# Moving 58 raw weight loads from SyncE's DMA queue to GpSimd's in a one-core attention and two-network kernel

## The chip, the core and the metric

The kernel runs on one NeuronCore of a Trainium2 chip. The core has a matrix engine (TensorE, in the rows PE), a vector engine (VectorE, DVE), an activation engine (ScalarE, ACT), a general engine (GpSimd, POOL) and SyncE (SP), which in this kernel only issues DMA transfers. Each engine takes its own instructions in order. The metric is the device time of one execution in microseconds (us); lower is better.

## What is computed

Three stages follow one another. Inputs are float32, except that the scaled weights come as float64 and are read by the kernel as pairs of 32-bit words.

```python
# attention: batch 4, 8 heads, 768 positions, head size 64, chunks of 32 with 16 left and 8 right
scores = q_c @ concat(mem_k, k_ctx).T / sqrt(64);  a = softmax(scores);  x = a @ concat(mem_v, v_ctx)
# first network: 3072 tokens, 512 -> 2048 -> 512
h = x @ w_in;  g = h * tanh(softplus(h));  x = g @ w_out
# second network: 3072 tokens, 512 -> 1536 -> 512
xn = x / sqrt(mean(x * x) + 1e-6) * rms_g
out = (silu(xn @ w_gate) * (xn @ w_val)) @ w_out2
```

## The kernel before

All large products are split into a high and a low part of each operand (three matmuls for one product), and most are done by a seven-product block scheme, a `group`. In the text the stages go by the lines of the matmuls:

- to about 300 us: attention, with the first products against `w_in` (`unit`, `group1`, matmuls L639 to L641) woven between its pieces; its results go to `g_scratch` in device memory;
- 300 to 378 us: the rest of `group1`;
- 378 to 645 us: `out1` (matmuls L754 to L756) reads `g_scratch` back through a `Feed` (load L771, activation L782) and multiplies by `w_out`;
- 645 to 985 us: `group2` (L639 to L641 with 512 columns), 36 groups against `w_gate` and `w_val`; operands `T` come from `nt_scratch` (L628), results `s` go to `h_scratch` (L111, through `store_later`);
- from 985 us: `group3` (L909 to L911) against the last `w_out2`.

Within a `group`, ScalarE copies the first bank into a tile `c` (L649), VectorE adds banks into it (L654, L665, L668, L670), and GpSimd adds the last quarter (L669) from `c` and a copy of another bank (L657). The pool of `c` tiles in `group2` has two buffers, so L649 of one group waits until L669 of an earlier one has read the tile.

The weights are converted on the fly by a generator, `cv_all`. A raw tile of 512 KB is loaded by `load_raw` (the DMA is line L149), two words for each value. ScalarE takes both halves (L202, L205), VectorE assembles the value (L209, L210, L216), and the value is split into high and low parts (L153 on ScalarE, L154 on VectorE, or on GpSimd for the rows of `w_out`). The pool `raw` has two buffers: the load of part n + 2 waits until L210 has read part n. `cv_prefetch` asks for the next load as soon as a part is done.

There are 74 such loads. The 16 of kind "half" (`w_in` for the first groups, before 123 us) are issued by GpSimd. The other 58 (6 of `w_in` and 24 of `w_gate` and `w_val`, kind "col"; 28 rows of the two `w_out` arrays, kind "row") are issued by SyncE, in one queue with everything else: attention operands, stores and reloads of `g_scratch`, `nt_scratch`, `h_scratch` and of the converted weights (`wi`, `wg`, `wo`). The order of the instructions on each engine is set by a scheduler that simulates the program; code that is marked with `pin` keeps its program order.

Of the kernel before, what the change touches and what calls it, by code (L numbers as in the profile page):

```python
# [29 lines left out]
def tile_kernel(  # L30
# [15 lines left out]
    nc = tc.nc  # L46
# [89 lines left out]
    def load_raw(arr, kind, f):  # L136
        raw = rawp.tile([128, 512, 2], I32, tag="raw", name="raw")
        if kind == "col":
            src = arr[:, f * 128:(f + 1) * 128].rearrange("(k p) f -> p k f", p=128).bitcast(I32)
            dst = raw.rearrange("p (k f) t -> p k (f t)", k=KC)  # L140
        elif kind == "half":
            i, half = f
            src = arr[256 * half:256 * half + 256, 256 * i:256 * i + 256]
            src = src.rearrange("(k p) f -> p k f", p=128).bitcast(I32)
            dst = raw.rearrange("p (k f) t -> p k (f t)", k=2)
        else:
            src = arr[f * 128:(f + 1) * 128, :].bitcast(I32)
            dst = raw.rearrange("p f t -> p (f t)")
        (nc.gpsimd if kind == "half" else nc.sync).dma_start(out=dst, in_=src)  # L149
        return raw  # L150

    def split(src, hi, lo, eng=None, keep=lambda ins: ins):
# [28 lines left out]
    def cv_prefetch(done):  # L181
        flat = [part for job in jobs for part in job[2]]
        while n_load[0] < min(len(flat), n_raw[0]) and n_load[0] - done < 2:
            raws.append(load_raw(*flat[n_load[0]]))
            n_load[0] += 1
# [1099 lines left out]
```

## Time and profile before

| | us |
|---|---|
| median of 3 runs | 1170.4 |
| lowest and highest of them | 1167.4 to 1171.19 |
| profiled execution, its time | 1169.38 |
| profiled execution, span of its instructions | 1167.6 |
| TensorE busy in the span | 1144.3 |
| VectorE, ScalarE, GpSimd busy | 824.7, 619.6, 180.2 |

The span runs from the first to the last instruction that the profile shows; 1.8 us of the execution's time lie around it. Busy time counts instructions that work; issuing a DMA from SyncE does not count. Releasers of waits are inferred. A TensorE clock of 1.00 in a row is the upper of its two levels (2.4 GHz), 0.5 the lower (1.2 GHz), and a value between is a mean over both.

### The profile page before, as it was taken

What the parts mean: (1) busy time and instruction counts of PE and PEld (TensorE: products, weight loads), DVE (VectorE), ACT (ScalarE), POOL (GpSimd) and SP (SyncE); (2) the same over time, 40 slices, a digit from 0 to 9 for tenths busy, and PEclk for the clock granted to TensorE, in tenths of its full rate; (3) what the DMA queues carried; (4) which work ended last, traced back from release to release, by engine and by line L of the source; (5) the groups of instructions that cost most, each with busy time, mean ns of one, the idle gap of its engine ahead of it and who ended that gap; (6) DMA issues with size and microseconds to landing.
All of it is one profiled execution on the core that took longest, in us unless ns stands there. A gap on an engine that the chain in (4) does not pass through costs nothing.

```text
span 1167.6 us, 22949 instructions
## 1 busy us (share of the span) xinstructions
PE 1144.3 (98%) x9052; PEld 1009.6 (86%) x9052; DVE 824.7 (71%) x1254; ACT 619.6 (53%) x1000; POOL 180.2 (15%) x165
## 2 busy tenths in 40 slices
PE   6899999999999999999999999999999999999998
PEld 4789999999999888888888788888888888999998
DVE  3655798844745876785775755978896857888883
ACT  4566666533545876676674433544454433444441
POOL 2011222310132311011011111111111111000000
PEclk9799999999999999999999999999999999999999
DMA  9889799899488774586599388999899889655431
GB/s 197 176 228 222 184 296 263 235 308 284 159 295 297 257 225 154 181 342 200 175 385 364 157 335 304 336 413 392 306 361 369 304 286 329 193 151 145 145 91 37
DMA packets 213276, 294.20 MB, mean 252 GB/s; under 512 B 104240, under 2 KB 160560, under 8 KB 204336
## 3 DMA queue, kind: packets, MB, share of 16 engines
q1 hardware_dynamic: 210864, 284.34, 73.7%
q0 software_dynamic: 2304, 8.39, 2.3%
q8 instruction: 71, 1.16, 0.4%
q14 instruction: 37, 0.30, 0.1%
HBM read 181.80 MB, written 110.89 MB: 251 GB/s over the span
## 4 chain that ended last, share of the span: by engine, by line
PE 90%; DVE 5%; ACT 2%; DMA 1%; issue 1%; POOL 0%; SPq 0%; ACTq 0%; DVEq 0%; POOLq 0%
PE bk L639 14%; PE bk L640 13%; PE bk L641 13%; PE bk L755 5%; PE bk L756 5%; PE bk L754 5%; PE bk L910 4%; PE bk L911 4%; PE bk L909 4%; PE bkp L639 2%; PE bkp L640 2%; PE bkp L641 2%; PE bkp L755 2%; PE bkp L756 2%; PE bkp L754 2%; PE bkp L457 1%
## 5 line engine op out<-in xcount | busy, mean ns | idle before, releaser
L639 PE MATMUL bk<-T,w 128*128 128x384 f32 (+1 forms) x860 | 315.4, 370 | 2.7 <-ACT s L747 2.1
L640 PE MATMUL bk<-T,w 128*128 128x384 f32 (+1 forms) x860 | 311.4, 362 | 0.0
L641 PE MATMUL bk<-T,w 128*128 128x384 f32 (+1 forms) x860 | 308.1, 362 | 0.0
L639 PEld LDWEIGHTS bk<-T,w 128*128 128x128 f32 x860 | 162.1, 189 | 22.2 <-ACT s L747 2.5
L640 PEld LDWEIGHTS bk<-T,w 128*128 128x128 f32 x860 | 162.2, 189 | 16.5 <-DVE T L154 0.3
L641 PEld LDWEIGHTS bk<-T,w 128*128 128x128 f32 x860 | 161.8, 188 | 15.6
L910 PE MATMUL bk<-w,T 128*128 128x256 f32 x396 | 112.0, 283 | 0.0
L911 PE MATMUL bk<-w,T 128*128 128x256 f32 x396 | 112.0, 283 | 0.0
L909 PE MATMUL bk<-w,T 128*128 128x256 f32 x396 | 112.0, 283 | 0.0
L755 PE MATMUL bk<-T,w 128*128 128x512 f32 x276 | 107.6, 390 | 0.2 <-DVE T L154 0.2
L756 PE MATMUL bk<-T,w 128*128 128x512 f32 x276 | 107.1, 389 | 0.0
L754 PE MATMUL bk<-T,w 128*128 128x512 f32 x276 | 106.7, 389 | 0.0
L669 POOL TENSOR_TENSOR v<-c,v 128x512 f32<-128x512 f32 x36 | 52.2, 1449 | 294.6 <-DVE c L665 235.8
L665 DVE TENSOR_TENSOR c<-bk,c 128x512 f32<-128x512 f32 (+2 forms) x72 | 43.1, 599 | 58.0 <-PE bk L641 45.5
L154 DVE TENSOR_TENSOR T<-s,T 128x1024 fp32r<-128x1024 f32 (+1 forms) x50 | 62.7, 1263 | 29.0 <-ACT T L153 28.9
L649 ACT COPY c<-bk 128x512 f32<-128x512 f32 (+2 forms) x72 | 37.0, 515 | 78.1 <-POOL v L669 32.7
L909 PEld LDWEIGHTS bk<-w,T 128*128 128x128 f32 x396 | 76.0, 192 | 0.1
L910 PEld LDWEIGHTS bk<-w,T 128*128 128x128 f32 x396 | 76.0, 192 | 0.1
L911 PEld LDWEIGHTS bk<-w,T 128*128 128x128 f32 x396 | 76.0, 192 | 0.0
L782 ACT ACTIVATE s<-s 128x1024 f32<-128x1024 f32 x44 | 46.5, 1059 | 33.1 <-DMA s<-g_scratch 33.1
L755 PEld LDWEIGHTS bk<-T,w 128*128 128x128 f32 x276 | 51.8, 188 | 11.4 <-DVE T L154 0.6
L756 PEld LDWEIGHTS bk<-T,w 128*128 128x128 f32 x276 | 51.8, 188 | 10.8
(226 smaller groups left out, 2282.3 us busy)
## 6 DMA issues: line engine op xcount, KB each, us to landing
T<-nt_scratch SPq DMA_DIRECT2D x35, 1024.0 KB
g_scratch<-g SPq DMA_DIRECT2D x64, 384.0 KB
s<-g_scratch SPq DMA_DIRECT2D x46, 512.0 KB
h_scratch<-s SPq DMA_DIRECT2D x36, 512.0 KB
w<-wg SPq DMA_DIRECT2D x10, 1792.0 KB
wg<-w SPq DMA_DIRECT2D x30, 512.0 KB
raw<-in_moe_w_out_dram SPq DMA_DIRECT2D x28, 512.0 KB
nt_scratch<-T SPq DMA_DIRECT2D x14, 1024.0 KB
```

Of the source, the lines that this page charges most:

```text
L154: keep((eng or nc.vector).tensor_tensor(lo, src, hi.bitcast(F32), op=ALU.subtract))
L639: nc.tensor.matmul(ps, whi, xh, start=first and kk == 0, stop=False, **more)
L640: nc.tensor.matmul(ps, whi, xl, start=False, stop=False, **more)
L641: nc.tensor.matmul(ps, wlo, xh, start=False, stop=kk == 1, **more)
L669: nc.gpsimd.tensor_tensor(c22, u3, z5, op=ALU.add)
L754: nc.tensor.matmul(ps, ahi, bhi, start=start, stop=False)
L755: nc.tensor.matmul(ps, ahi, blo, start=False, stop=False)
L756: nc.tensor.matmul(ps, alo, bhi, start=False, stop=stop)
L782: nc.scalar.activation(x, g, self.act)
L909: nc.tensor.matmul(ps, t[:, 0, f], w[:, 0], start=first and f == 0, stop=False, **more)
L910: nc.tensor.matmul(ps, t[:, 0, f], w[:, 1], start=False, stop=False, **more)
L911: nc.tensor.matmul(ps, t[:, 1, f], w[:, 0], start=False, stop=f == HG - 1, **more)
```

## The change

Every raw load is now issued by GpSimd; nothing else in the source differs.

```diff
@@ load_raw @@
         else:
             src = arr[f * 128:(f + 1) * 128, :].bitcast(I32)
             dst = raw.rearrange("p f t -> p (f t)")
-        (nc.gpsimd if kind == "half" else nc.sync).dma_start(out=dst, in_=src)
+        nc.gpsimd.dma_start(out=dst, in_=src)
         return raw
```

So 58 instructions leave SyncE's queue and enter GpSimd's, where the scheduler places them. On SyncE, in the middle of `out1`, two loads of raw weights stood among the reloads of `g_scratch` (L771) and the stores of converted weights (L111 `wg<-w`):

```order
 L771 DMA s<-g_scratch 128x2x512 x2
 L111 DMA wg<-w 128x1024 x2
-L771 DMA s<-g_scratch 128x2x512
-L149 DMA raw<-in_moe_w_gate_dram 128x4x256
-L771 DMA s<-g_scratch 128x2x512 x2
-L149 DMA raw<-in_moe_w_val_dram 128x4x256
-L771 DMA s<-g_scratch 128x2x512
+L771 DMA s<-g_scratch 128x2x512 x4
 L111 DMA wg<-w 128x1024
 L771 DMA s<-g_scratch 128x2x512
```

What moved: the two L149 are gone, and the four L771 follow each other directly. On GpSimd in `group2`, from the last sums of squares (L824, L825) on, the 36 L669 stood alone; the first rows of what stands there now are these (`v` is the tile with the group's last quarter):

```order
 L825 TENSOR_TENSOR w<-w 128x512
-L669 TENSOR_TENSOR v<-c,v 128x512 x36
+L669 TENSOR_TENSOR v<-c,v 128x512 x8
+L149 DMA raw<-in_moe_w_gate_dram 128x4x256
+L149 DMA raw<-in_moe_w_val_dram 128x4x256
+L149 DMA raw<-in_moe_w_gate_dram 128x4x256
+L669 TENSOR_TENSOR v<-c,v 128x512
+L149 DMA raw<-in_moe_w_val_dram 128x4x256
+L669 TENSOR_TENSOR v<-c,v 128x512
+L149 DMA raw<-in_moe_w_gate_dram 128x4x256
+L149 DMA raw<-in_moe_w_val_dram 128x4x256
+L669 TENSOR_TENSOR v<-c,v 128x512
```

What moved: 24 loads now stand between the L669, one or two behind each of most of them from the eighth on. On VectorE the same instructions stand in a slightly different order from about 735 us to 925 us; the first such place (L209, L210 and L216 assemble a value, L668, L654 and L749 belong to a group) is:

```order
 L670 SCALAR_TENSOR_TENSOR v<-bk_85,c 128x512
-L668 TENSOR_TENSOR s<-bk_84,s 128x512
-L749 TENSOR_TENSOR s<-s,v 128x1024
-L216 ISA ca<-ca,lr 128x1024
-L210 SCALAR_TENSOR_TENSOR ca<-raw,ca 128x512
-L654 TENSOR_TENSOR s<-bk_87,c 128x512
+L209 TENSOR_SCALAR ca<-ca 128x512
+L668 TENSOR_TENSOR s<-bk_84,s 128x512
+L749 TENSOR_TENSOR s<-s,v 128x1024
+L216 ISA ca<-ca,lr 128x1024
+L654 TENSOR_TENSOR s<-bk_87,c 128x512
+L210 SCALAR_TENSOR_TENSOR ca<-raw,ca 128x512
```

What moved: L210, which frees a raw tile, stands behind L654 instead of ahead of it, and L209 comes a little later. TensorE's matmuls of two neighbouring groups are interleaved in another order in the same stretch; before 735 us only a handful of rows on any engine but SyncE and GpSimd differ.

## Rows read from the trace of the kernel before

**Rows 1.** The page: span, and busy time of each engine.
```profile
span 1167.6 us, 22949 instructions
PE 1144.3 (98%) x9052; PEld 1009.6 (86%) x9052; DVE 824.7 (71%) x1254; ACT 619.6 (53%) x1000; POOL 180.2 (15%) x165
```

**Rows 2.** Stages: stretch and length, busy us of PE, PEld, DVE, ACT, POOL, clock, DMA.
```profile
122.00:300.00 178.00, 177.57 (x2654) 163.88 (x2654) 129.41 (x244) 95.34 (x184) 35.84 (x39) 1.00 0.87 256
300.00:378.00 78.00, 78.00 (x434) 75.34 (x432) 49.44 (x80) 42.52 (x73) 22.41 (x18) 1.00 0.75 259
378.00:645.00 267.00, 266.02 (x1172) 219.61 (x1172) 193.08 (x249) 185.55 (x233) 38.52 (x26) 1.00 0.72 256
645.00:985.00 340.00, 337.32 (x1492) 279.02 (x1491) 253.26 (x381) 150.86 (x262) 50.96 (x36) 0.99 0.86 324
985.00:1165.00 180.00, 178.37 (x1487) 178.16 (x1485) 133.31 (x171) 72.57 (x112) 12.17 (x13) 1.00 0.46 136
```

**Rows 3.** TensorE's waits from 122 us on: total us, times, longest us.
```profile
PE bk L639 <- ACT s L747: 2.1, 1, 2.1
PE bk L639 <- ACT c L657: 0.6, 1, 0.6
PE bkp L639 <- ACT v L657: 0.6, 1, 0.6
PE bk L489 <- ACT p L476: 0.4, 1, 0.4
...
PE bk L755 <- DVE w L154: 0.2, 1, 0.2
```

**Rows 4.** Waits of SyncE's queue at the raw loads, the largest.
```profile
SPq L149 <- DVE ca L210: 101.7, 40, 7.8
```

**Rows 5.** The raw loads' line: issue time, ns min/median/max; landing times of GpSimd's.
```profile
L149 SPq DMA_DIRECT2D raw<-in_moe_w_out_dram x28: 332/333/1416, 208.2 to 911.0; - x28
L149 POOL DMA_DIRECT2D raw<-in_moe_w_in_dram x16: 722/722/847, 3.1 to 122.3; - x16
L149 SPq DMA_DIRECT2D raw<-in_moe_w_gate_dram x12: 372/383/384, 401.8 to 790.9; - x12
...
DMA to landing us min/median/max: 4.3/5.4/7.2
```

**Rows 6.** Waits on both sides of L669: total us, times, longest us.
```profile
POOL v L669 <- DVE c L665: 235.8, 29, 16.8
...
ACT c L649 <- POOL v L669: 32.7, 8, 7.0
```

**Rows 7.** Raw loads beside L669 in `group2`: start and length in us.
```profile
833.26 4.17 SPq L149 DMA_DIRECT2D raw<-in_moe_w_out_dram  x2
868.60 0.33 SPq L149 DMA_DIRECT2D raw<-in_moe_w_out_dram  x1
...
833.97 1.31 POOL L669 TENSOR_TENSOR v<-c,v 128x512 f32<-128x512 f32 x1 [2.79 <-DVE c L665]
867.80 1.57 POOL L669 TENSOR_TENSOR v<-c,v 128x512 f32<-128x512 f32 x1 [8.31 <-DVE c L665]
...
878.48 0.66 ACT L202 ACTIVATE ca<-raw 128x512 f32<-128x512 f32 x1 [2.54 <-DMA raw<-in_moe_w_out_dram]
```

**Rows 8.** Stages of five us around TensorE's longest wait, columns as in rows 2.
```profile
660.00:665.00 5.00, 2.88 (x14) 2.06 (x12) 5.00 (x7) 3.01 (x4) 0.00 (x0) 1.00 0.24 96
665.00:670.00 5.00, 5.00 (x15) 3.98 (x16) 5.00 (x7) 2.99 (x5) 0.00 (x0) 0.66 0.44 175
```

**Rows 9.** VectorE beside an addition, and beside a raw load, on GpSimd: start, length.
```profile
400.09 1.67 DVE L210 SCALAR_TENSOR_TENSOR ca<-raw,ca 128x512 int32<-128x512 int32 x1
399.63 1.58 POOL L154 TENSOR_TENSOR w<-ca,w 128x512 fp32r<-128x512 f32 x1 [2.24 <-ACT w L153]
...
81.51 0.68 DVE L216 CUSTOM_DVE_ANT_0 ca<-ca,lr 128x1024 uint16<-128x1024 uint16 x1
81.55 0.72 POOL L149 DMA_DIRECT2D raw<-in_moe_w_in_dram  x1 [5.33 <-DMA raw<-in_moe_w_in_dram]
```

## The prediction

> **What bounds the kernel now.** I read the page first, for how much time TensorE does not work. It is busy for 1144.3 of 1167.6 us [rows 1], so 23.3 us are all that any edit can give back without making matmuls faster. Next come the stages, for where those 23.3 us lie. From 122 to 985 us, in which all 58 moved loads are issued (the sixteenth load of GpSimd's starts at 122.3, SyncE's last at 911.0 [rows 5]), TensorE is idle for 0.43 + 0 + 0.98 + 2.68 = 4.1 us, and in the stage behind it for another 1.6 [rows 2]. The remaining 17.6 us lie before 122 us or after 1165 us, where the change touches nothing. Third come TensorE's own waits from 122 us on, to see who ended those 4.1 us: 2.1 us in one piece, two of 0.6, one of 0.4, and no row of the view, from the first to the last, names a DMA [rows 3]. So no transfer, raw load or other, makes TensorE wait directly. VectorE is the next engine, with 253.26 of 340 us in `group2` [rows 2]; GpSimd is at 50.96 there. The kernel is bound by matmuls, and the stretch that the change touches is the one where they are closest to gapless.
>
> **The change part by part.**
>
> *Off SyncE.* 58 issues leave, at 0.33 us (28 of them) and 0.38 (the 24 of `w_gate` and `w_val` and, by the same shape, the 6 of `w_in`), together 28 x 0.33 + 30 x 0.38 = 20.6 us, and with them the waits in front of them: 101.7 us on L210 alone, over 40 loads, 7.8 at the longest [rows 4, 5]. Each of those waits held whatever stood behind it in SyncE's queue: stores, reloads of `g_scratch`, operands `T`. This is the part that could gain. But what stood behind ends on no row of TensorE's waits, so I cost the gain on the path at nothing. The cover is the prefetch distance of these transfers; it is given by TensorE's not waiting for one of them in 863 us, and an earlier issue can only lengthen it. The upper end of the gain is the 4.1 us of rows 2, of which the largest piece is bound otherwise (below).
>
> *Onto GpSimd.* The 16 loads that it issues already take 0.72 us each, with a median and a minimum alike and 0.85 at the most [rows 5]. They are of 256 pieces of 2 KB; the row loads are of 128 pieces of 4 KB, the column loads of 512 of 1 KB, and the trace has neither on this queue. If the time went with the pieces, they would take 0.36 and 1.44; if it is fixed, 0.72. I take 0.72, since minimum and median agree, and the range of the sum is 28 x 0.36 + 30 x 0.72 = 32 us to 28 x 0.72 + 30 x 1.44 = 63 us, with 42 as my value. GpSimd then works 222 us instead of 180.2, under a fifth of the span. What hides it is its own idle time: in `group2` 340 - 51 = 289 us [rows 2], against 24 loads of 0.72, 17 us.
>
> *The new waits on GpSimd.* A load waits there for the raw tile, that is mostly for L210 on VectorE, as it did on SyncE. Behind it now stand L669, the L154 of the `w_out` rows, and the sums L823 to L825; behind L669 wait L649 on ScalarE (the tile `c`) and L749 on VectorE. What matters is whether a load stands ahead of an L669 that could already run. L669 itself waits for VectorE, 235.8 us in all for L665 [rows 6]; so both wait for the same engine, and if the scheduler has them in VectorE's order, the load costs L669 only its issue. I laid the old times against the new order. The load issued at 868.60 now stands ahead of the L669 that began at 867.80: held 868.60 + 0.72 - 867.80 = 1.5 us [rows 7]. The pair of loads begun at 833.26 now stands behind the L669 of 833.97 and loses 833.97 + 1.31 - 833.26 = 2.0 us, on a tile with a conversion or more of time before it is read. I found no larger hold of an L669 than the first. Against that stands how much TensorE can bear: ScalarE's L649 already waits for L669, 8 times and for 32.7 us, once for 7.0 [rows 6], and TensorE has no wait that goes back to it at that length; its waits on ScalarE in rows 3 are 2.1 and shorter. So a hold of 1.5 us is covered more than four times, and I cost the move at nothing on the path, with 0 at the lower end and at the upper end what the first rival gives.
>
> *The transfers themselves.* The bytes and the sixteen engines stay. The load issued at 868.60 was waited for until ScalarE started at 878.48, so it landed 9.9 us after its issue among the transfers of SyncE's queue [rows 7]; GpSimd's landed after 4.3 to 7.2 us, median 5.4, in the first stages [rows 5]. I expect the moved ones nearer to the second. That frees ScalarE for a few us, not TensorE: 0 again, with a gain of at most one of the pieces of 0.6.
>
> *Could a busy VectorE starve the issue?* The rows say: while GpSimd issued a load at 81.55, a VectorE instruction from 81.51 took 0.68, and the load its 0.72; while GpSimd added (L154, from 399.63, 1.58 long), VectorE's L210 from 400.09 took 1.67 [rows 9]. So additions on GpSimd and VectorE's work with two inputs stand in each other's way for about 1 us, and issues do not, in those rows. The Trainium skill ("SBUF — State Buffer", SBUF: two separate sides) warns of just this change: a DMA issued by GpSimd has its descriptors written by that engine, which is locked out while VectorE holds the port that both share, so it should go over SyncE's or ScalarE's queue instead. By the row the sum stays 1169.9; by the rule each issue would be longer by a VectorE instruction, and the sum would move only where that makes a hold too long (the second rival).
>
> *The other order.* From about 735 to 925 us VectorE's and TensorE's instructions stand in another order. The sums are the same; the waits there may differ. In the old order they were a small part of 2.68 us, and 2.1 of it (the one long wait) is before 735, so the new order starts from about 0.6 us of waits, and I take the same, with 0 and one long wait more as the ends.
>
> **The sum.** 1169.38 us of the profiled execution, less 0, plus 0. That execution lies 1.0 under the median of 1170.4, so I predict between the two, 1169.9 us.
>
> **The rivals.**
>
> *Slower: GpSimd's queue is held up.* If the real order of VectorE does not match the simulated one, a load that waits as long as on SyncE, 7.8 us [rows 4], then issues for 0.72, holds L669 for 8.5. That is 1.5 over the 7.0 that is borne; from 7.0 on it decides. The price of a hold on TensorE is more than the wait: behind the one long wait, which ended just before 665, the granted clock was 0.66 over 5 us, a mixture of the lower of its two levels and the upper, a loss of 5 x 0.34 = 1.7 us [rows 8]. So such an event costs 1.5 + 1.7 = 3.2 us. Two of them give 1176; a single one in which the whole 2.1 us of rows 3 is repeated gives 1169.9 + 2.1 + 1.7 = 1173.7. Against it: the holds that I could work out are 2 us or less. Chance 0.14, and 0.05 for the same price from the other order on VectorE alone.
>
> *Slower: the issue is starved.* As a mechanism of this kernel: an issue is lengthened by the 1.0 us by which L210 was lengthened in rows 9, so the hold becomes 9.5, and the event 2.5 + 1.7 = 4.2 us; two give 1178. The Trainium skill's page "SBUF — State Buffer" would have it so. Against it: 16 issues of 0.72 to 0.85, in stages where VectorE was less loaded. Chance 0.04.
>
> *Faster: SyncE's queue was the hidden cause.* All waits from 122 to 985 us vanish, with the low clock: 4.1 + 1.7 = 5.8 us, 1164. For it: 101.7 us of waits in that queue. Against it: the longest wait is for ScalarE's L747, in a stretch from 650 on in which the raw tiles serve the last operand and SyncE has no raw load at all, and VectorE is busy for 5.00 of 5 us right there [rows 8]. Without it 2.0 us remain, within what counts as no change. Chance 0.10.
>
> *The change does not do what it says* can't be: the order shows the loads on the other engine.
>
> **How the numbers follow.** A measurement of this kernel can't tell less than about 0.3%, 3.5 us, from no change. No change has 0.67, with 1166.4 to 1173.4 as its own range; slower 0.14 + 0.05 + 0.04 = 0.23; faster 0.10. For 8 in 10 the range runs from 1166 (which leaves out most of the faster case) to 1176 (two holds).
>
> **What would show it.** Right: GpSimd's L149 about 0.7 us each and GpSimd near 220 us busy; the waits of SyncE's queue shorter by some 100 us; TensorE's busy time and idle time from 122 to 985 us within 2 us of 1144 and 4.1; the wait before 665 still there; L649's wait for L669 about as before. Wrong: a TensorE wait released by ScalarE's L649 or L657 behind an L669 that stood behind a load, with a clock under 1.00 after it; L149 on GpSimd well over 1.4 us; or the wait before 665 gone.

## The result: about 1% slower

| | median us | lowest to highest | ratio to the kernel before, 95% interval |
|---|---|---|---|
| before (in the first and the second measurement) | 1170.03, 1170.19 | 1166.92 to 1172.96 | |
| after, first measurement (6 runs) | 1181.54 | 1175.98 to 1184.29 | 1.0097 [1.0078, 1.0116] |
| after, second measurement (5 runs) | 1180.27 | 1178.93 to 1181.15 | 1.0084 [1.0070, 1.0099] |

The prediction was 1169.9 us, no change, with a range of 1166 to 1176. The change costs 10 to 11.5 us. The page of the kernel after (first measurement, an execution of 1182.16 us) in the lines that answer to [rows 1], with the DMA queues (q1 carries what SyncE issues, q0 what GpSimd issues: packets, MB, share of the sixteen engines' time) and the engines' shares of the chain that ended last:

```profile
span 1180.4 us, 22955 instructions
PE 1146.5 (97%) x9052; PEld 1009.9 (86%) x9052; DVE 820.1 (69%) x1254; ACT 619.1 (52%) x1000; POOL 218.7 (19%) x223
...
q1 hardware_dynamic: 190992, 253.93, 65.3%
q0 software_dynamic: 10656, 38.80, 10.1%
...
PE 82%; DMA 8%; DVE 6%; ACT 3%; issue 1%; POOL 0%; SPq 0%; DVEq 0%; ACTq 0%; POOLq 0%
```

TensorE's busy time hardly changed, and GpSimd's 218.7 us are what was forecast. New is what stands in the chain: DMA has 8% of it; in the chain of before it had 1%. Before, q0 carried 8.39 MB and q1 284.34; the 30.4 MB of the 58 raw loads moved from the one to the other.

The stages, columns as in [rows 2]:

```profile
122.00:300.00 178.00, 177.51 (x2655) 163.93 (x2654) 129.30 (x245) 95.62 (x184) 42.56 (x47) 1.00 0.89 257
300.00:378.00 78.00, 77.57 (x430) 74.75 (x429) 47.94 (x78) 42.14 (x72) 27.02 (x27) 1.00 0.74 252
378.00:645.00 267.00, 262.47 (x1148) 216.79 (x1147) 192.28 (x250) 183.05 (x227) 49.12 (x42) 0.99 0.70 246
645.00:985.00 340.00, 332.13 (x1454) 273.23 (x1453) 240.96 (x370) 146.42 (x256) 65.97 (x60) 0.99 0.85 321
```

TensorE's idle time in these four is 0.49 + 0.43 + 4.53 + 7.87 = 13.3 us, where [rows 2] had 4.1. TensorE's waits there, as in [rows 3]:

```profile
PE bk L639 <- ACT c L657: 4.6, 2, 4.3
PE bkp L639 <- DMA T<-nt_scratch: 3.2, 2, 2.4
PE bk L639 <- DMA T<-nt_scratch: 2.5, 1, 2.5
PE bk L639 <- ACT s L747: 2.1, 1, 2.1
```

The 2.1 us of [rows 3] are still there, as forecast. The other three rows are most of the loss, and two of them name what no row of [rows 3] named: a DMA, the load of an operand `T` by SyncE (L628). They lie at three places.

**Near 380 us**, at the start of `out1`. A row of the chain (start, length), and a row each of ScalarE's and TensorE's timeline (in brackets the idle time before the instruction, and what ended it):

```profile
374.23 8.06 DMA w<-g_scratch
...
382.31 1.06 ACT L782 ACTIVATE sm<-w 128x1024 f32<-128x1024 f32 x1 [4.76 <-DMA w<-g_scratch]
...
383.79 0.69 PE L639 MATMUL bk<-T,w 128*128 128x384 f32 x1 [4.30 <-ACT c L657]
```

The reload of `g_scratch` into the tile `w` (L771) takes 8.06 us from its issue; before it took 4.26. ScalarE's L782 waits for it, L657 stands next in ScalarE's queue (it starts at 383.28), and TensorE waits 4.30 us for L657. The 5 us that follow (columns as in [rows 2]) run at a clock of 0.56, which costs another 2.2 us:

```profile
385.00:390.00 5.00, 5.00 (x15) 4.13 (x14) 3.19 (x5) 4.09 (x7) 4.69 (x4) 0.56 0.36 133
```

**Near 770 us**, in `group2`: the operands' loads on SyncE's queue, the raw loads on GpSimd's, and TensorE behind them.

```profile
757.48 3.18 SPq L628 DMA_DIRECT2D T<-nt_scratch  x3
...
760.32 0.77 POOL L149 DMA_DIRECT2D raw<-in_moe_w_gate_dram  x1 [1.19 <-ACT ca L202]
764.75 0.77 POOL L149 DMA_DIRECT2D raw<-in_moe_w_val_dram  x1
...
773.20 0.50 PE L639 MATMUL bk<-T,w 128*128 128x512 f32 x1 [2.53 <-DMA T<-nt_scratch]
...
757.48 15.68 DMA T<-nt_scratch
```

The load of `T` issued at 757.48 is waited for until 773.20, 15.68 us in the chain. The same place in the kernel before (which is some 7 us ahead when `group2` begins), on SyncE's queue alone, and the stretches of it that hold this place and the next (columns as in [rows 2]):

```profile
749.50 1.90 SPq L628 DMA_DIRECT2D T<-nt_scratch  x2
752.34 0.38 SPq L149 DMA_DIRECT2D raw<-in_moe_w_gate_dram  x1
756.03 1.13 SPq L628 DMA_DIRECT2D T<-nt_scratch  x2
758.20 1.12 SPq L149 DMA_DIRECT2D raw<-in_moe_w_val_dram  x1
...
760.00:800.00 40.00, 40.00 (x179) 33.12 (x178) 27.62 (x44) 17.49 (x32) 4.16 (x3) 1.00 1.03 414
870.00:900.00 30.00, 29.44 (x130) 24.07 (x129) 20.24 (x35) 14.38 (x27) 2.59 (x2) 1.00 1.01 409
```

There the raw load of 752.34 stands behind two loads of `T`, and that of 758.20 behind two more. The last two rows are what I had not asked for: from 760 to 800 and from 870 to 900 us the sixteen DMA engines were fully taken already, at 414 and 409 GB/s, so whatever is served earlier is served at the cost of something else.

**From 882 to 889 us**, in the next round of operands, the two waits on `bkp`: 0.84 and 2.37 us.

How far the program had come at four points (starts of the first and last matmuls of the lines named, in us; L639 multiplies in the first network's groups and in `group2`, L754 to L756 in `out1`, whose first products stand among the last of `group1`, from 322.7 us on before; L909 in `group3`) gives the loss by stage, for every kernel that was run:

| profiled execution of | its time | first L639 | to first L754 | `out1`, to last L756 | `group2`, to first L909 |
|---|---|---|---|---|---|
| before | 1169.38 | 45.3 | 277.4 | 310.7 | 347.0 |
| after | 1182.16 | 46.3 | 277.0 | 317.3 | 352.9 |
| after, second measurement | 1180.45 | 46.1 | 279.0 | 314.3 | 352.9 |
| `w_out` only | 1177.29 | 45.4 | 277.9 | 316.0 | 347.8 |
| `w_gate`, `w_val` only | 1172.79 | 45.5 | 276.8 | 311.6 | 350.2 |
| `w_out2` only | 1172.71 | 44.8 | 276.7 | 311.3 | 351.6 |
| issue only | 1173.63 | 45.4 | 277.9 | 311.5 | 349.9 |
| all but `w_out` | 1175.68 | 45.0 | 276.5 | 311.2 | 354.8 |
| operands too | 1197.53 | 45.3 | 278.9 | 318.4 | 364.8 |
| operands and reloads too | 1188.97 | 45.5 | 277.9 | 317.6 | 358.1 |
| eleven back | 1173.76 | 47.2 | 277.2 | 312.9 | 347.1 |
| `w_in`, `w_out` only | 1170.29 | 45.7 | 277.5 | 313.3 | 345.4 |
| `w_val` only | 1169.18 | 44.6 | 276.9 | 312.1 | 347.3 |
| `w_out2` by ScalarE | 1175.29 | 46.0 | 277.8 | 310.8 | 351.8 |

Single executions of one kernel differ by some 4 us either way, so one row of this table settles nothing by itself; the ratios below do, with the waits at the places named.

### The profile page after: what moved, and what is told of

It is laid out like the page before. It is cut to its first block, busy times and chain, and to the rows that moved or that the text cites. A ratio compares the mean times of both kernels' runs of the same rounds, so it can differ in the third digit from the quotient of the medians.

```text
span 1180.4 us, 22955 instructions
## 1 busy us (share of the span) xinstructions
PE 1146.5 (97%) x9052; PEld 1009.9 (86%) x9052; DVE 820.1 (69%) x1254; ACT 619.1 (52%) x1000; POOL 218.7 (19%) x223
## 3 DMA queue, kind: packets, MB, share of 16 engines
q1 hardware_dynamic: 190992, 253.93, 65.3%
q0 software_dynamic: 10656, 38.80, 10.1%
## 4 chain that ended last, share of the span: by engine, by line
PE 82%; DMA 8%; DVE 6%; ACT 3%; issue 1%; POOL 0%; SPq 0%; DVEq 0%; ACTq 0%; POOLq 0%
PE bk L639 12%; PE bk L640 12%; PE bk L641 12%; PE bk L755 5%; PE bk L756 5%; PE bk L754 5%; PE bk L909 4%; PE bk L911 4%; PE bk L910 4%; DMA T<-nt_scratch 3%; PE bkp L754 2%; PE bkp L755 2%; PE bkp L639 2%; PE bkp L756 2%; PE bkp L640 2%; PE bkp L641 2%
## 5 line engine op out<-in xcount | busy, mean ns | idle before, releaser
L639 PE MATMUL bk<-T,w 128*128 128x384 f32 (+1 forms) x860 | 316.1, 370 | 9.4 <-ACT c L657 4.6
L640 PE MATMUL bk<-T,w 128*128 128x384 f32 (+1 forms) x860 | 311.6, 362 | 0.0
L639 PEld LDWEIGHTS bk<-T,w 128*128 128x128 f32 x860 | 162.3, 189 | 29.9 <-ACT c L657 5.2
L909 PE MATMUL bk<-w,T 128*128 128x256 f32 x396 | 112.2, 283 | 0.1
L756 PE MATMUL bk<-T,w 128*128 128x512 f32 x276 | 107.1, 389 | 0.0
L754 PE MATMUL bk<-T,w 128*128 128x512 f32 x276 | 106.4, 389 | 0.0
L665 DVE TENSOR_TENSOR c<-bk,c 128x512 f32<-128x512 f32 (+2 forms) x72 | 43.0, 598 | 68.9 <-PE bk L641 56.6
L669 POOL TENSOR_TENSOR v<-c,v 128x512 f32<-128x512 f32 x36 | 51.1, 1420 | 214.4 <-DVE c L665 160.1
L154 DVE TENSOR_TENSOR T<-s,T 128x1024 fp32r<-128x1024 f32 (+1 forms) x50 | 62.4, 1256 | 29.1 <-ACT T L153 29.0
L649 ACT COPY c<-bk 128x512 f32<-128x512 f32 (+2 forms) x72 | 36.9, 514 | 75.5 <-POOL v L669 26.4
L909 PEld LDWEIGHTS bk<-w,T 128*128 128x128 f32 x396 | 76.0, 192 | 0.4 <-ACT T L153 0.3
L782 ACT ACTIVATE s<-s 128x1024 f32<-128x1024 f32 x44 | 46.5, 1060 | 34.2 <-DMA s<-g_scratch 33.9
L755 PEld LDWEIGHTS bk<-T,w 128*128 128x128 f32 x276 | 51.8, 188 | 11.5 <-DVE T L154 0.6
L756 PEld LDWEIGHTS bk<-T,w 128*128 128x128 f32 x276 | 51.8, 188 | 10.9
```

What stands on the lines that cost most here:

```text
L154: keep((eng or nc.vector).tensor_tensor(lo, src, hi.bitcast(F32), op=ALU.subtract))
L639: nc.tensor.matmul(ps, whi, xh, start=first and kk == 0, stop=False, **more)
L640: nc.tensor.matmul(ps, whi, xl, start=False, stop=False, **more)
L669: nc.gpsimd.tensor_tensor(c22, u3, z5, op=ALU.add)
L754: nc.tensor.matmul(ps, ahi, bhi, start=start, stop=False)
L755: nc.tensor.matmul(ps, ahi, blo, start=False, stop=False)
```

## The experiments

**The theories.** A: a raw load that stood in SyncE's queue was served behind the operands issued before it. On a queue of its own it is served beside them, in stretches where the DMA engines are full, and the transfer that TensorE or ScalarE needs next lands later by that much. B: GpSimd's issues and waits hold L669 and L154 up (my first two rivals). C: the scheduler's other order does it. D: it is a property of GpSimd's queue, not of a second queue as such.

Where nothing else is said, an experiment changes only the line of `load_raw` that the change touched; the sixteen `half` loads stay with GpSimd in all of them.

### Only the rows of `w_out`

```diff
-        nc.gpsimd.dma_start(out=dst, in_=src)
+        (nc.gpsimd if kind == "half" or arr is w_out else nc.sync).dma_start(out=dst, in_=src)
```

> Of the 58 moved loads only the row loads of w_out (16 of the 28 rows) go over GpSimd's queue; the loads of w_gate, w_val and w_out2 stay on SyncE's. The scheduler's order on ScalarE is then that of before, and TensorE's differs in about 50 lines. Theory A (a raw load on a queue of its own no longer stands behind SyncE's earlier transfers, and is served beside or ahead of them): the reload of g_scratch that is waited for near 380 us lands late again, TensorE idles some 4 us there and runs at the lower clock for some 7 us more, so about 6 to 7 us over before, 1176.5 (ratio 1.005 to 1.006); the waits on T<-nt_scratch near 770 and 885 us are not there. Theory B (GpSimd's issues and waits hold L669 and L154 up): a sixth of the loads in a stage with few L669, so 1170 to 1172, with no wait of over 1 us near 380. Theory C (the scheduler's other order does it): the order is nearly that of before, so 1170.

Measured: median 1169.52 us, ratio 1.0004 [0.9988, 1.0019]. The profiled execution, 1177.29, is the slowest of twelve (the others 1167.66 to 1172.85), and it has the stall, in the chain and in TensorE's timeline:

```profile
374.32 7.67 DMA w<-g_scratch
...
383.48 0.44 PE L639 MATMUL bk<-T,w 128*128 128x384 f32 x1 [3.98 <-ACT c L657]
```

So the place is the one that theory A named and nothing came up at 770 or 885 us, but the size was missed: by the times the stall comes in few executions, and the median of this part alone is not slower. TensorE's instructions stand in the order of before until behind this place, so its own order (theory C) did not make the stall. (The 16 rows are 28% of the 58 loads, not the sixth that the expectation has.)

### Only the columns of `w_gate` and `w_val`

```diff
-        nc.gpsimd.dma_start(out=dst, in_=src)
+        (nc.gpsimd if kind == "half" or arr is w_gate or arr is w_val else nc.sync).dma_start(out=dst, in_=src)
```

> Only the 24 column loads of w_gate and w_val go over GpSimd's queue. Theory A: no stall near 380 us; TensorE waits some 2.5 us for T<-nt_scratch near 770 us, where two raw loads of 512 KB are served beside the operands, so 1172 to 1174 (ratio 1.002 to 1.004). Theory B: most loads in the stage with most L669, so more than half of the 11.5 us, 1176 or over, with waits of ScalarE's L649 for L669 longer than the 7.0 of before. Theory C: the order of the stage from 645 us on differs, 1175 or over without any wait for T<-nt_scratch.

Measured: 1173.87 us, 1.0028 [1.0016, 1.0041]. TensorE, near 770 us of the kernel after:

```profile
764.36 0.50 PE L639 MATMUL bk<-T,w 128*128 128x512 f32 x1 [2.04 <-DMA T<-nt_scratch]
```

As theory A has it, with 2.04 us at the place and no stall near 380 us. In the next round of operands TensorE waits 0.83, 0.68 and 0.82 us more for `T`, which no theory had named. The raw loads of that round are on SyncE's queue here, but at other places in it: SyncE issues them behind the second and the fourth load of `T` (raw loads at 865.14 and 868.19; `T` at 862.88, at 864.62, and two from 866.74), where before they stood behind the fourth and the sixth. So the scheduler's order of one queue can put raw loads ahead of operands too; that this is what cost the 2.3 us is argued, and no run tested it.

### Only the rows of `w_out2`

```diff
-        nc.gpsimd.dma_start(out=dst, in_=src)
+        (nc.gpsimd if kind == "half" or arr is w_out2 else nc.sync).dma_start(out=dst, in_=src)
```

> Only the 12 row loads of w_out2 go over GpSimd's queue. Theory A: no stall near 380 nor near 770 us; TensorE waits some 3 us for T<-nt_scratch near 885 us, so 1172 to 1174 (ratio 1.002 to 1.004). Theory B: 12 issues of 0.55 us cost nothing that can be measured, 1170. Theory C: the order from about 735 us on differs, so 1173 to 1176 with no wait for T<-nt_scratch.

Measured: 1172.06 us, 1.0015 [1.0002, 1.0028]. This is the cleanest pair, since up to this place the execution keeps the times of before within 1 us. First the kernel before, SyncE's queue (its raw load of 868.60 is in [rows 7]), then this one, SyncE's queue, GpSimd's, TensorE, and the chain:

```profile
865.13 0.33 SPq L149 DMA_DIRECT2D raw<-in_moe_w_out_dram  x1
871.04 0.32 SPq L628 DMA_DIRECT2D T<-nt_scratch  x1
```

```profile
862.60 7.18 SPq L628 DMA_DIRECT2D T<-nt_scratch  x5
...
865.04 0.74 POOL L149 DMA_DIRECT2D raw<-in_moe_w_out_dram  x1 [6.12 <-DVE ca L210]
867.15 0.55 POOL L149 DMA_DIRECT2D raw<-in_moe_w_out_dram  x1 [1.37 <-ACT w L153]
...
875.07 0.50 PE L639 MATMUL bkp<-T,w 128*128 128x512 f32 x1 [2.62 <-DMA T<-nt_scratch]
...
861.30 13.73 DMA T<-nt_scratch
```

The raw loads are issued at 865.04 and 867.15, where they were issued at 865.13 and 868.60, and the last load of `T` 1 us earlier than before (the five end by 869.78; before the last began at 871.04). No `T` was issued later (the one waited for, the second of the round, at 861.30; before at 861.87), and yet TensorE waits 2.62 us for it, where before it did not wait. TensorE's instructions stand in the order of before until about 886 us, so its own order (theory C) did not make this wait. What changed about these transfers is the queue on which the two raw loads stood, and the trace has what the queues moved from 868 to 876 us, before and then here (packets, MB, share of the sixteen engines' time):

```profile
q1 hardware_dynamic: 536, 3.43, 102.0%
...
q1 hardware_dynamic: 386, 2.25, 69.6%
q0 software_dynamic: 285, 1.04, 32.0%
```

Before, SyncE's queue had the engines for itself. Here the two raw loads, 1.04 MB, took 32% of 8 us, 2.6 us, while TensorE waited for a load of `T` that had been issued 4 and 6 us ahead of them. That is theory A's mechanism in numbers.

### The issue on GpSimd, the bytes on SyncE

```diff
-        nc.gpsimd.dma_start(out=dst, in_=src)
+        for q_, lo, hi in ((nc.gpsimd, 0, 8), (nc.sync, 8, None)) if kind != "half" else ((nc.gpsimd, 0, None),): q_.dma_start(out=dst[..., lo:hi], in_=src[..., lo:hi])
```

> GpSimd issues all the moved loads and waits for their raw tiles as after the change, but each of them moves only the first 8 words of every piece; SyncE's queue issues the rest of the bytes, as before. Theory A: the bytes stand behind SyncE's earlier transfers again, so the waits on T<-nt_scratch near 770 and 885 us and the stall near 380 us shrink to under 1 us each: 1170 to 1173 (ratio 1.000 to 1.003). Theory B: GpSimd's issues and waits are those of after, so 1180 to 1183 (ratio 1.0097).

Measured: 1172.20 us, 1.0019 [1.0004, 1.0034]. GpSimd is busy for 216.7 us and its L149 take as long as after, so theory B's cost is all there, and about four fifths of the loss are gone. The reload near 380 us and TensorE's waits from 645 us on:

```profile
373.23 4.42 DMA w<-g_scratch
...
PE bk L639 <- ACT s L747: 2.7, 2, 2.1
PE bk L639 <- DVE c L665: 1.6, 2, 0.8
```

No wait for `T` is left; 4.42 us for the reload is nearly the 4.26 of before. The 1.6 us for VectorE's L665 are two waits of 0.79, which may be the other order or the doubled loads. Theory B falls. Theory C does not fall by this run, since the scheduler's order here is another again; against it stands the run before, with TensorE's old order and the wait.

### The change again, and all but `w_out`

The first is the changed kernel itself; the second:

```diff
-        nc.gpsimd.dma_start(out=dst, in_=src)
+        (nc.sync if arr is w_out else nc.gpsimd).dma_start(out=dst, in_=src)
```

> The changed kernel itself, once more and on the chip of the other runs of this call. The parts alone added 0.04, 0.28 and 0.15%, 5.5 us together, but the whole 11.5. Theory A1 (the rest is the stall near 380 us, which came in the profiled execution of the w_out part but in none of the other eleven, and comes more often with all parts moved): the times fall into two clusters, one near 1175.5 and one 6 to 7 us above it, with the upper one the more frequent. Theory A2 (the rest is an interaction that is there each time): one cluster near 1181.5. Theory A3 (the chip of the first measurement was another): a median near 1176.

> All moved loads go over GpSimd's queue but the 16 rows of w_out, which stay on SyncE's. Theory A (order of service, place by place): no stall near 380 us, the waits for T<-nt_scratch near 770 and 885 us are there, so 1175 to 1176.5 (ratio 1.004 to 1.0055). If the rest of the loss is an interaction elsewhere than near 380 us: 1180 or over.

Measured: 1180.27 us, 1.0084 [1.0070, 1.0099], five runs within 2.3 us of each other, so one cluster; and 1176.61 us, 1.0049 [1.0031, 1.0068], as theory A had it (1.78 + 1.06 us for `T` near 770, 2.90 near 885, none near 380). The guess of two clusters (A1) fell: the second profiled execution of after, 1180.45 us, has no 4 us stall near 380 (its longest wait between 300 and 400 us is 0.99), but the waits in `group2` again, the last of them now on ScalarE's L205:

```profile
771.91 0.50 PE L639 MATMUL bk<-T,w 128*128 128x512 f32 x1 [2.40 <-DMA T<-nt_scratch]
882.21 0.50 PE L639 MATMUL bkp<-T,w 128*128 128x512 f32 x1 [1.11 <-DMA T<-nt_scratch]
887.45 0.47 PE L639 MATMUL bkp<-T,w 128*128 128x512 f32 x1 [2.19 <-ACT lr L205]
```

Both executions have `group2` at 352.9 us. In `out1` the second lost 3.6 us, with no single wait of TensorE's over 1 us.

### The operands on GpSimd's queue too, and the reloads

```diff
-            nc.sync.dma_start(out=t.bitcast(F32), in_=dram[:, p - 1].bitcast(F32))
+            nc.gpsimd.dma_start(out=t.bitcast(F32), in_=dram[:, p - 1].bitcast(F32))
```

and, in the second kernel, also

```diff
-                nc.sync.dma_start(out=g, in_=self.source(*self.steps[self.nl]))
+                nc.gpsimd.dma_start(out=g, in_=self.source(*self.steps[self.nl]))
```

> As after the change, but the loads T<-nt_scratch of L628 are issued by GpSimd too, so that raw loads and operands stand in one queue again. Theory A: the waits for T<-nt_scratch near 770 and 885 us are gone, the stall near 380 us stays where it comes, so 5 to 6 us under after, 1175 to 1177; near 1170 in executions without that stall. Theory B (GpSimd's queue is held up): a load of T waits there for its tile, L669 behind it is held longer, so 1182 to 1186.

> As the kernel with T<-nt_scratch on GpSimd's queue, and the reloads of g_scratch (L771) there too, so that everything that TensorE waits for after 380 us stands in one queue with the raw loads, and only stores and the loads of other stages are on SyncE's. Theory A: all three stalls gone, 1168 to 1172. Theory B: more waits on GpSimd's queue, L154 and L669 held, 1182 or over.

Measured: 1189.53 us, 1.0174 [1.0141, 1.0207], and 1188.22 us, 1.0163 [1.0137, 1.0188]. Both numbers of theory A missed, by 12 us and more, and those of theory B (over 1182) were nearer. But the traces do not show B's mechanism, an L669 held by a load. In the first kernel no row of TensorE's waits names `T` any more, as A had it; the longest wait is another. ScalarE, TensorE and the chain there:

```profile
957.11 1.02 ACT L153 CAST w<-ca 128x256 fp32r<-128x256 f32 x3 [5.07 <-DMA wo<-w]
...
958.66 0.80 PE L639 MATMUL bkp<-T,w 128*128 128x512 f32 x1 [5.70 <-ACT v L657]
...
940.83 16.18 DMA wo<-w
```

Now a store of converted weights (`wo<-w`, L111 on SyncE) is late, 16.18 us; ScalarE's L153 waits for its slot, L657 stands behind it, and TensorE waits 5.70 us. ScalarE's L649 waits 33.2 us for L669, 8 times and 7.0 at the longest, which is what [rows 6] had. While the store was under way, from 941 to 957 us, GpSimd's queue had 61.9% of the sixteen engines' time. Read so, it is theory A's mechanism with the sides changed: what stayed on SyncE's queue is now served beside what left it. That is argued from this trace, and no further run tested it. It is also one wait of several: another of 3.65 us, at 864.24, ends on ScalarE's L649 behind an L153 that had waited 3.86 us for VectorE, not for a transfer, and near 380 us TensorE waits 3.47 us behind a reload of 7.22. The second kernel still has 2.00 us for `T` and 2.23 for a converted weight (`w<-wg`), and near 380 us, where reload and raw loads now stand in one queue, a wait of 3.24 us on ScalarE's L153. So theory A does not account for the 8 to 9 us that these two kernels take beyond the changed one.

### Eleven of the 58 back on SyncE's queue

```diff
-        nc.gpsimd.dma_start(out=dst, in_=src)
+        back = arr is w_out and f in (9, 10, 11) or (arr is w_gate or arr is w_val) and f in (8, 9) or arr is w_out2 and f in (3, 9, 4, 10); (nc.sync if back else nc.gpsimd).dma_start(out=dst, in_=src)
```

> As after the change, but eleven of the 58 moved loads go back to SyncE's queue: the three rows of w_out that were issued nearest to 372 us, the four columns of w_gate and w_val issued from 744 to 765 us, and the four rows of w_out2 issued from 860 to 877 us; 47 stay on GpSimd's. Theory A (only a raw load that is served beside a transfer that is needed at once costs anything): the stall near 380 us and the waits for T<-nt_scratch near 770 and 885 us go, 1170 to 1173 (ratio 1.000 to 1.003). Theory B (GpSimd's issues and waits) or any cost that goes with the number of loads on that queue: 47/58 of the loss stays, 1178 to 1180.

Measured: 1172.54 us, 1.0028 [1.0014, 1.0041]: with a fifth of the loads back, two thirds of the loss are gone. The stages that hold the places at 770 and 885 us, columns as in [rows 2]:

```profile
760.00:800.00 40.00, 40.00 (x178) 32.96 (x177) 30.19 (x48) 18.13 (x34) 6.67 (x7) 1.00 1.02 411
870.00:900.00 30.00, 29.45 (x130) 24.04 (x129) 22.41 (x38) 12.45 (x25) 5.27 (x5) 1.00 1.01 407
```

TensorE is busy for 40.00 and 29.45 us of them, as before the change (40.00 and 29.44), and `group2` takes 347.1 us (347.0 before), with 20 loads of `w_gate` and `w_val` and 8 of `w_out2` still on GpSimd's queue. That excludes, for `group2`, a cost that goes with the number of loads. It does not tell theory A from theory C, since with these eleven back the scheduler also gives TensorE nearly the order of before: between 645 and 950 us only six matmuls stand elsewhere. What is left lies in `out1` and ahead of it.

### `w_in` and `w_out` only

```diff
-        nc.gpsimd.dma_start(out=dst, in_=src)
+        (nc.gpsimd if arr is w_in or arr is w_out else nc.sync).dma_start(out=dst, in_=src)
```

> The six column loads of w_in and the 16 rows of w_out go over GpSimd's queue, the 36 others stay on SyncE's. It asks where the w_out part gets its 4 us from, which it has in company with all others and not alone. If from w_in (both are loaded before 410 us, and a load of w_in that is issued a little later or earlier shifts the w_out rows against the reload of g_scratch): 1174 to 1176 (ratio 1.003 to 1.005). If it needs the loads behind it (w_gate and w_val from 408 us on), or is the stall that comes in some executions only: 1169 to 1171, with a single one higher.

Measured: 1171.28 us, 1.0022 [1.0004, 1.0041], between the two expectations; one execution of twelve took 1178.47. The profiled one has a wait of 2.06 us for L657 near 380, behind a reload of 5.74 us. Inconclusive: with the run of `w_out` alone, this part costs between nothing and 0.4%.

### Only the columns of `w_val`

```diff
-        nc.gpsimd.dma_start(out=dst, in_=src)
+        (nc.gpsimd if kind == "half" or arr is w_val else nc.sync).dma_start(out=dst, in_=src)
```

> Only the 12 column loads of w_val go over GpSimd's queue, half of those of w_gate and w_val. Here the order of TensorE's instructions differs from before in 29 lines only. Theory A: the bytes served beside the operands near 770 us are halved, one raw load of 512 KB in place of two, so the wait for T<-nt_scratch there is 0.5 to 1.5 us instead of 2.4, and the time 1170.5 to 1172.5 (ratio 1.0005 to 1.002). Theory C (the scheduler's other order): the order of before, so 1170 and no such wait.

Measured: 1169.96 us, 1.0007 [0.9993, 1.0020]. The interval holds a halved dose as well as nothing, and the wait is not the one I named; TensorE near 770 us, and the chain there:

```profile
769.05 0.50 PE L639 MATMUL bk<-T,w 128*128 128x512 f32 x1 [1.54 <-ACT s L747]
...
754.11 14.21 DMA h_scratch<-s
```

A store of `h_scratch` took 14.21 us, and ScalarE's L747 waited for its tile; a raw load of 0.52 MB was served on GpSimd's queue in that time. So a late transfer again, but of another kind than theory A named, where TensorE had lost nothing before. VectorE's and ScalarE's orders differ more than TensorE's here, and this run does not tell their part in it from that of the queue.

### The rows of `w_out2` on ScalarE's queue

```diff
-        nc.gpsimd.dma_start(out=dst, in_=src)
+        (nc.gpsimd if kind == "half" else nc.scalar if arr is w_out2 else nc.sync).dma_start(out=dst, in_=src)
```

> Only the 12 row loads of w_out2 are moved, and to ScalarE's queue instead of GpSimd's; GpSimd's order is that of before. Theory A in its general form (any queue but SyncE's takes the raw loads out from behind the operands): TensorE waits 2 to 3 us for T<-nt_scratch near 885 us, as in the kernel with these loads on GpSimd's queue, 1172 or over; over that as far as the loads' own waits hold ScalarE up. Theory D (it is GpSimd's queue of software descriptors that does it): no wait for T<-nt_scratch of over 0.5 us near 885 us.

Measured: 1175.36 us, 1.0054 [1.0040, 1.0068]. The queue (a row of its own, hardware), the issues on it, and TensorE:

```profile
q10 hardware_dynamic: 1728, 6.29, 1.5%
...
882.72 0.80 PE L639 MATMUL bk<-T,w 128*128 128x512 f32 x1 [3.79 <-DMA T<-nt_scratch]
```

The wait for `T` is there again, 3.79 us, with GpSimd's order that of before and 12 issues of 0.33 us each. From 870 to 878 us the ScalarE queue moved 1.05 MB, two raw loads, in 35.2% of the engines' time, 2.8 us. The rest of the 3.79 can come from the load of `T` itself, issued at 866.91 where before it was at 864.09, though the execution was only 1.1 us behind. Theory D falls: a second queue does it, whoever issues on it.

## Why the prediction was wrong

**Onto GpSimd, and could a busy VectorE starve the issue: right.** L149 on GpSimd, as in [rows 5]:

```profile
L149 POOL DMA_DIRECT2D raw<-in_moe_w_out_dram x28: 545/560/634, 205.3 to 925.3; - x28
L149 POOL DMA_DIRECT2D raw<-in_moe_w_gate_dram x12: 766/767/921, 408.2 to 804.1; - x12
```

0.56 us for 128 pieces, 0.77 (`w_val` 0.75) for 512: the time hardly goes with the pieces, and no issue took more than 0.92. Both lie inside the bounds of 0.36 and 1.44, and the 42 us were 38.5.

**The new waits on GpSimd: right.** ScalarE's L649 waited 26.4 us for L669, 7 times, the longest 7.0 again [rows 6]. The rival of a held queue did not come, and neither did the starved issue.

**Off SyncE: no gain, as costed, but wrong in what would be seen.** The 101.7 us of [rows 4] are gone, but not 100 us of the queue's waiting: over all its rows it is 860.6 us after and 823.6 before. What stood behind the raw loads waits itself now, the stores for L749 72.6 us (33.9 before) and those for L154 97.1 (67.9).

**The transfers themselves: this is the step that failed.** It said: "The bytes and the sixteen engines stay", and "That frees ScalarE for a few us, not TensorE: 0". Both halves were read from rows, and the conclusion does not follow. With engines that are full, as in `group2` at 770 and 885 us, the order in which the bytes are served is what a queue decides, and the raw loads left theirs. They do land sooner after their issue, in a median of 4.7 to 6.4 us, as I expected; what they gained was taken from `T`, the reload of `g_scratch` and the stores. As an estimate, two raw loads of 0.524 MB at 414 GB/s are 2 x 1.27 = 2.5 us, and the wait near 770 us is 2.53. The step's measured size, in place of 0: 5.9 us in `group2` (both executions of after), of which 2.53 + 0.84 + 2.37 = 5.74 are the waits for `T` in the first. There the runs show the cause: only `w_out2` (no `T` later, TensorE in its old order, and the raw loads served in that time) and ScalarE's queue; issue only and eleven back agree, but they change the scheduler's order too.

In `out1` the loss is 3.6 to 6.6 us, and the cause is shown less well. In the profiled executions the stall near 380 us goes with the queue of `w_out`'s bytes. A wait of over 2 us for L657 is there in four of the five with all of these rows on GpSimd's queue and the reload on SyncE's (4.30, 3.98, 3.47 and 2.06 us; 0.82 in the second of after), and in none of the eight with them, or with the three nearest, on SyncE's (0.57 to 0.89). But the sixteen engines were not full there (share 0.72 from 376 to 378 us after the change), so the sum with the stretch's GB/s does not explain it.

The Trainium skill (DMA: Bandwidth & Descriptors, "Queues, rings and completion order") states the rule that was missing: each DMA engine takes turns between the queue rows for which it has work. The runs agree with it, on GpSimd's queue (2.62 us) and on ScalarE's (3.79). By that rule and the 414 GB/s of the stretch a rival could have been worked out.

**The cover was misread in the same step and under "Off SyncE".** I took "TensorE's not waiting for one of them in 863 us" for a prefetch distance that an earlier issue can only lengthen. A row that is absent says that a margin is over zero, not how large it is; near 770 and 885 us it was, by the same estimate, under 2.5 us.

**The other order: not refuted.** With the order changed and the bytes back (issue only) 1.6 us of waits for L665 remain; with eleven loads back none do, but there the order is nearly the old one. No run has the order of after with the bytes on SyncE's queue.

**What stays open.** The parts add up to less than the whole: all but `w_out` 0.49%, `w_out` with or without `w_in` 0.04 to 0.22, the whole 0.84 to 0.97. The intervals leave between nothing and some 5 us of this. In the second execution of after it lies ahead of 645 us in pieces of at most 1 us, in whose chain stand reloads `s<-g_scratch`, raw loads and a store of `nt_scratch`. I tested none of them by itself. Why the reload near 380 us takes 8 us in some executions and 4.5 in others is open too.

## What to carry to other kernels

Moving a DMA to another engine's queue moves it out from behind the transfers that stood ahead of it there: look at the DMA share of the stretch first, and where it is near 1.00, estimate the price of the move as the moved bytes over the stretch's GB/s, against each transfer that an engine needs within that time. A missing wait row is no margin; find it by the landing time of the transfer against the start of its first reader. And where a queue costs something at a few places only, as here at three, putting the few transfers of these places back can be enough; here that took most of the loss away, and brought the scheduler's order nearly back as well, though no kernel of these beat the one before (the nearest, `w_out` only and `w_val` only, are at 1.0004 and 1.0007).

## What the runs showed of the hardware that I had not expected

- **The median landing time on GpSimd's queue hardly depended on the bytes.** With 4 KB per load (issue only) it is 5.2 us, and with 16 KB 4.2 to 5.2, where the loads of 512 KB after the change took 4.7 to 6.4.
- **The same bytes in fewer packets.** The 30.4 MB were 19,872 packets on SyncE's queue (210,864 less 190,992) and are 8,352 on GpSimd's (10,656 less 2,304).
- **A wait costs twice, but not each time.** Around the end of the 4.30 us near 380 us the granted clock was 0.76 from 380 to 385 us and 0.56 from 385 to 390, means between its two levels; after the 2.53 us that ended at 773.20 it stayed at 1.00, the upper one. After the 2.62 us of the kernel with only `w_out2` moved it was 0.66 from 875 to 880 us.
